# Softmax sums in the stage before the feed-forward on 32-column tiles, reciprocals taken of one column per transposed block, and weights converted without a clamp

## Chip, core and metric

The kernel runs on one core of a Trainium2 chip. A core has five engines with instruction streams of their own: TensorE (PE in the profile, its weight loads PEld), VectorE (DVE), ScalarE (ACT), GpSimd (POOL) and SyncE (SP), which here issues almost all DMAs. PE writes its products to PSUM, eight banks of 128 partitions; GpSimd doesn't reach PSUM in this kernel. The metric is the device time of one execution in microseconds, the median of several runs; lower is better.

## What is computed

Attention with RMS-normalized queries and keys over 8 batches of 12 heads (448 positions, head size 64), then a feed-forward with a squared ReLU over the 3584 rows that result. q, k and v are float32; the feed-forward's weights are float64 and reach the kernel as 64-bit words.

```python
def _attn_ref(q, k, v, g_q, g_k):
    def rmsnorm(x, g):
        rms = np.sqrt(np.mean(x * x, axis=-1, keepdims=True) + 1e-06)
        return x / rms * g
    q_n, k_n = (rmsnorm(q, g_q), rmsnorm(k, g_k))
    scores = 1.0 / np.sqrt(q.shape[-1]) * np.matmul(q_n, k_n.transpose(0, 1, 3, 2))
    scores = scores - np.max(scores, axis=-1, keepdims=True)
    attn = np.exp(scores)
    attn = attn / (np.sum(attn, axis=-1, keepdims=True) + 1e-09)
    return np.matmul(attn, v).astype(np.float32)

def _moe_ref(x, w_in, w_out):          # x: 3584 x 768, d_ff 2048
    h = np.maximum(x @ w_in, 0.0)
    return (h * h @ w_out).astype(np.float32)
```

## The kernel before

**Pairs.** The attention goes by pairs of heads: 8 batches of 6 pairs, 48 in all, numbered i. A pair's two heads (e = 0, 1) lie side by side on the 128 partitions. Its 448 keys are three slots m = 0, 1, 2 of 128 and a last one (m = NJ) of 64; the last slots of an even and the following odd pair share one tile. For each slot `weigh` makes transposed scores on PE (L369) into banks 0 to 3, and ACT takes the exponential into a tile wT (L374). `attend` multiplies the weights by v into the values bank (L438). The sums of the weights over the keys come in one of two ways. For pairs with `alone(i)`, those of the first two batches, every slot is also multiplied by a matrix of ones of 64 columns (L445), so that the sum stands on all 64 partitions of a head. For the others POOL adds the slots up (`add_up`, L393) and `denominators` multiplies the result once by ones (L456); ACT copies that out of bank 3 (L460). `invert_half` takes reciprocals on DVE, each of 128 x 224 elements, two per pair (L475), and `finish` multiplies the values by them (L484).

**Inputs of a pair.** q and k are loaded as rows, three per partition 128 rows apart (`load_full`, L147); squares on ACT (L167), sums on DVE (L178, L181), a power on POOL (L187), the scaling of q on POOL (L202); `turn` transposes q and k on PE (L344, L347), then DVE writes qT (L352) and ACT kT (L354). From pair 14 on, q and k come in blocks that DVE transposes (`turn_blocks`, L315). With gains as small as here the exponentials need no maximum; the branch with `shift` is for the other case and isn't taken.

**Feed-forward.** Two batches at a time, u = 0 to 3, in products of sums of blocks: `first_products` (L602, to L622 to L624) and `second_products` (L683, L654), whose results DVE adds to accumulators (L724, L700). A product is accumulated in one of three banks by roles, `roles`.

**Order.** There is no scheduler: the order of emission is that of each engine's queue. The outer loop goes through visits, two (n = 0, 1) for each pair. The first 26 are `visit_alone`, with attention alone on PE. In the first of them attend of the previous pair comes first, then the scores of this one, then a transpose; in the second attend again, the sums of squares, a transpose of k, the reciprocals and `finish`, and the scores. From then on the feed-forward's generator runs, and `visit_among` is called at even distances between its products; small jobs wait in `tasks` and `pool_tasks` and are emitted one or two per product. Thus everything that DVE does for attention stands in one queue with L724.

**Weights.** They come in 64 pieces. A piece is loaded by SP into a tile `words` (three buffers), split on ACT (L784 to L786) and joined on DVE: `join_words` first clamps the high words to plus or minus MOST (L797), then shifts them (L801); `end_join` follows with L821 and L825. 16 pieces go with the visits alone (`begin`), the other 48 with the first feed-forward (`convert`). From there on the forms of the weights are kept in DRAM.

**Banks** of the stage alone: scores 0 to 3; values 4 or 5 and sums 6 or 7, by the pair's parity (`values_bank`, `sums_bank`); the transposes use 4 to 7 too. Among the feed-forward: values 4, sums 3, transposes 0, products 5 to 7.

**Buffers**: wT has eight, acc seven (2*NT+1), part four; the squares of the stage alone lie in acc tiles, later in one tile `squares`.

## Time and profile before

| | us |
|---|---|
| median of 3 runs | 1480.34 (1480.28 to 1481.03) |
| the profiled execution | 1483.94 |
| its span, first to last instruction | 1482.0 |

Busy time of the engines over the span, and the costliest groups that the change touches (instructions, busy us, mean ns of one):

| | count | busy us | mean ns |
|---|---|---|---|
| PE | 4932 | 1447.8 (98%) | |
| DVE | 1225 | 744.7 (50%) | |
| ACT | 1151 | 606.6 (41%) | |
| POOL | 509 | 611.2 (41%) | |
| L475 reciprocals, source in SBUF | 72 | 108.6 | 1531 |
| L475 reciprocals, source in PSUM, 20 to 147 us | 22 | 32.6 | 1523 |
| L445 ones-products, 20 to 147 us | 144 | 34.2 | 539 |
| L445 with ones_of, 20 to 147 us | 48 | 11.1 | 539 |
| L797 clamps, 147 to 520 us | 48 | 27.7 | 578 |

A busy time is the union of a group's spans, so instructions that overlap count once. PE at 98% doesn't mean PE at its best: its matmuls are pipelined and their ends are modelled, so its pace is read from the starts. A float32 product shows as two MATMUL records and two weight loads. A row of the timeline is a run of like instructions of one engine, with the start of the first, the time from there to the end of the last, the names (out<-in), the shape and the count. "128\*64" is the tile of the array: rows by columns. An arrow in brackets names what ended the idle time before an instruction.

### The profile page before, as it was taken

Reading aid. Unit: us, or ns where it says so; the run is one execution under the profiler, and the core shown is the slowest. Engines: PE = TensorE matmul, PEld = TensorE weight load, DVE = VectorE, ACT = ScalarE, POOL = GpSimd, SP = SyncE. Lnnn points to the kernel's source line nnn. Section 1 sums busy time; section 2 is a strip of 40 time slices with the busy share of each in tenths; the row PEclk is TensorE's granted clock in tenths of the full one; section 3 lists DMA queues with packets and bytes.
Section 4 is the critical chain, followed back from the end, with each engine's and each line's share of the span. In section 5 each row is a group of like instructions: output and inputs, shape, how many; then the busy total and the mean of one; then the engine's idle time right before and its main releaser. Section 6 shows DMA issues by size and latency. Waiting matters only on the chain.

```text
span 1482.0 us, 15262 instructions
## 1 busy us (share of the span) xinstructions
PE 1447.8 (98%) x4932; PEld 691.5 (47%) x4932; DVE 744.7 (50%) x1225; ACT 606.6 (41%) x1151; POOL 611.2 (41%) x509
## 2 busy tenths in 40 slices
PE   7999999989999999999999999999999999999998
PEld 3333444444344444545444454544445455555554
DVE  5987367888887652335244353324434261222323
ACT  6775565645546334351433325342332403222130
POOL 3434745654635735354353645435352342021111
PEclk9999999999999999999999999999999999999999
DMA  6665336555646563443444464253533214223122
GB/s 150 166 191 136 75 83 179 163 179 147 203 128 210 166 209 89 127 130 63 147 102 137 119 193 126 55 163 86 144 103 109 81 69 166 85 75 122 38 85 77
DMA packets 309278, 188.11 MB, mean 127 GB/s; under 512 B 265796, under 2 KB 293316, under 8 KB 300996
## 3 DMA queue, kind: packets, MB, share of 16 engines
q1 hardware_dynamic: 308384, 186.84, 43.2%
q8 instruction: 41, 0.67, 0.2%
q14 instruction: 49, 0.40, 0.1%
q10 hardware_dynamic: 804, 0.20, 0.1%
HBM read 144.57 MB, written 42.40 MB: 126 GB/s over the span
## 4 chain that ended last, share of the span: by engine, by line
PE 89%; DVE 6%; DMA 1%; issue 1%; ACT 1%; SPq 0%; DVEq 0%; ACTq 0%
PE bank L602 33%; PE bank L683 28%; PE bank L369 9%; PE bank L438 9%; PE bank L654 5%; PE bank L445 2%; PE bank L456 2%; DVE xT L475 1%; DVE acc L724 1%; PE bank L344 1%; DVE words L797 1%; DVE hid L622 1%; DVE in_sb L801 0%; DMA vt<-in_v_dram 0%; ACT wT L374 0%
## 5 line engine op out<-in xcount | busy, mean ns | idle before, releaser
L602 PE MATMUL bank<-xT,in_sb 128*128 128x448 f32 x1344 | 517.3, 542 | 0.0
L602 PEld LDWEIGHTS bank<-xT,in_sb 128*128 128x128 f32 x1344 | 251.8, 190 | 262.1 <-issue 253.0
L724 DVE TENSOR_TENSOR acc<-acc,bank 128x384 f32<-128x384 f32 x324 | 172.0, 545 | 246.3 <-PE bank L683 186.8
L374 ACT ACTIVATE wT<-bank,rr 128x448 f32<-128x448 f32 x336 | 188.1, 633 | 260.6 <-PE bank L369 254.2
L683 PE MATMUL bank<-out_sb,hid 128*128 128x384 f32 x768 | 269.8, 491 | 7.5 <-DVE acc L724 7.4
L187 POOL TENSOR_TENSOR rr<-ms,minus_half 128x16 f32<-128x16 f32 (+3 forms) x50 | 125.4, 2508 | 352.2 <-DVE ms L181 322.9
L683 PE MATMUL bank<-out_sb,sums 128*128 128x384 f32 x576 | 207.4, 496 | 6.2 <-DVE acc L724 6.2
L622 DVE TENSOR_TENSOR hid<-bank,part 128x448 f32<-128x448 f32 x128 | 76.9, 621 | 271.9 <-PE bank L602 270.2
L683 PEld LDWEIGHTS bank<-out_sb,hid 128*128 128x128 f32 x768 | 144.9, 191 | 117.1 <-DVE acc L724 12.7
L393 POOL TENSOR_TENSOR sum<-sum,wT 128x448 f32<-128x448 f32 (+1 forms) x144 | 164.6, 1165 | 16.0 <-ACT wT L374 13.3
L369 PE MATMUL bank<-qT,kT 64*128 64x448 f32 (+1 forms) x768 | 166.2, 573 | 3.0 <-ACT words L784 1.1
L623 ACT ACTIVATE hid<-hid 128x448 f32<-128x448 f32 x128 | 73.3, 573 | 203.1 <-DVE hid L622 203.1
L683 PEld LDWEIGHTS bank<-out_sb,sums 128*128 128x128 f32 x576 | 108.3, 192 | 93.4 <-DVE acc L724 14.2
L638 POOL TENSOR_TENSOR sums<-hid 128x384 f32<-128x384 f32 x32 | 32.4, 1013 | 286.9 <-ACT hid L624 286.5
L438 PE MATMUL bank<-wT,vt 128*64 128x448 f32 x576 | 130.1, 548 | 1.5 <-DMA vt<-in_v_dram 1.5
L609 ACT COPY part<-bank 128x448 f32<-128x448 f32 x128 | 67.7, 529 | 149.0 <-PE bank L602 148.8
L475 DVE RECIPROCAL xT<-xT 128x224 f32<-128x224 f32 x72 | 108.6, 1531 | 28.4 <-ACT xT L460 28.4
L369 PEld LDWEIGHTS bank<-qT,kT 64*128 64x128 f32 (+1 forms) x768 | 54.9, 173 | 103.5 <-issue 82.2
L393 POOL TENSOR_TENSOR sum<-wT 128x448 f32<-128x448 f32 x72 | 83.6, 1181 | 45.8 <-PE bank L456 45.8
L178 DVE TENSOR_REDUCE ms<-squares 128x8 f32<-128x512 f32 (+1 forms) x68 | 41.9, 617 | 119.6 <-ACT squares L167 119.6
L654 PE MATMUL bank<-out_sb,hid 128*128 128x384 f32 x256 | 86.4, 491 | 0.0
L624 ACT ACTIVATE hid<-hid 128x448 f32<-128x448 f32 x128 | 73.8, 577 | 4.0
(70 smaller groups left out, 1115.4 us busy)
## 6 DMA issues: line engine op xcount, KB each, us to landing
out_sb<-out_forms SPq DMA_DIRECT2D x24, 1536.0 KB, 7.8
in_sb<-in_forms SPq DMA_DIRECT2D x24, 1344.0 KB, 5.9
words<-in_moe_w_in_dram SPq DMA_DIRECT2D x32, 384.0 KB, 3.6
words<-in_moe_w_out_dram SPq DMA_DIRECT2D x32, 384.0 KB, 3.4
out_forms<-out_sb SPq DMA_DIRECT2D x8, 1536.0 KB, 6.5
in_forms<-in_sb SPq DMA_DIRECT2D x8, 1344.0 KB, 5.7
qk<-in_q_dram SPq DMA_DIRECT2D x96, 96.0 KB, 3.2
vt<-in_v_dram SPq DMA_DIRECT2D x96, 96.0 KB, 3.4
```

Source lines behind the costliest of these rows:

```text
L187: self.nc.gpsimd.tensor_tensor(out=self.rr[i][:, first : first + number, 0 : self.count(i)], in0=ms, in1=self.minus_half[:, :, None].to_br ...
L369: nc.tensor.matmul(sc[some], lhsT=turned[p, 1][r, keys], rhs=turned[p, 0][r, :], start=True, stop=True,)
L374: nc.scalar.activation(new_weights((i, m), e), sc, AF.Exp, scale=rows.rr[i][:, 1, 2 * m + e : 2 * m + e + 1],)
L393: nc.gpsimd.tensor_tensor(out=sums[i, e][some], in0=left[some], in1=weights[key_of(i, m), e][some], op=ALU.add)
L438: nc.tensor.matmul(values_bank(i)[ds(e * D, D), :], lhsT=lasts[i % 2][some, e, :] if mine else values[i][:, m, e, :], rhs=weights[key, e][ ...
L475: nc.vector.reciprocal(out=dens[i][:, some], in_=den[:, some])
L602: nc.tensor.matmul(ps, lhsT=w_sb[:, IN.index(left), c, :], rhs=forms[u, c][right], start=first and c == 0, stop=c == NK - 1, skip_group_ch ...
L622: nc.vector.tensor_tensor(out=dst, in0=left, in1=right, op=op)
L624: nc.scalar.activation(dst, dst, AF.Square)
L654: nc.tensor.matmul(ps, lhsT=flat[a][:, t, ds(NT * P, P)], rhs=w_sb[t][:, 2 * a + half, :], start=(a, t) == parts[0], stop=(a, t) == parts[-1],
L683: nc.tensor.matmul(ps, lhsT=lefts[left][:, t, ts(tt, P)], rhs=w_sb[t][:, OUT.index(right), :], start=first and t == 0, stop=t == 1, skip_g ...
L724: nc.vector.tensor_tensor(out=acc, in0=acc, in1=ps, op=ALU.add)
```

## The change

Before the feed-forward the ones-products have 32 columns. The sums' bank then has four tiles of 32 partitions: for each head one that takes the first two slots in turn by their parity and one for the other parity. `attend` and the ones-products are separate functions now and go slot after slot; `visit_alone` emits scores first, then transposes, then the previous pair's products, and the pair's values always go to bank 4, its sums to bank 5, its transposes to 6 and 7. The weights of slots 0 and 1 of pairs alone lie in part and acc tiles, and the second square of such a pair is POOL's.

Reciprocals: DVE transposes the sums in blocks of 32 by 32 into a tile `inverse` (with the tag and the one buffer of `squares`), so that column 0 of each block holds 32 positions' sums on 32 partitions. Where the sums are in two parts, four copies of 32 partitions and an addition bring them together. The reciprocal is taken of 14 columns, and a transpose of its broadcast fills `inverse`, by which `finish` multiplies. Among the feed-forward the same is done after `denominators`, whose copy on ACT goes; transposing stands there at once, the rest is a task.

For pairs whose k isn't loaded in blocks, k and v are loaded with three adjacent rows on each partition (`in_chunks`). The clamp before the shift of the high words is left out. At the start of the first feed-forward two products are emitted ahead of the visit, and the roles of the banks begin in the order 7, 6, 5.

```diff
         ]
-    def go_on(self, io, small):
+        self.in_blocks = lambda i: False
+    def go_on(self, io, small, in_blocks):
+        other.in_blocks = in_blocks
         return other
+    def in_chunks(self, i, some):
+        if self.in_blocks(i):
+            return some.rearrange("(j p) d -> p j d", p=P)
+        return some.rearrange("(p j) d -> p j d", j=NJ)
...
     def load_full(self, i, x, queue):
         b, c = divmod(i, self.H // 2)
         for e in range(2):
+            some = self.qk[x][b, 2 * c + e, 0 : NJ * P]
             queue.dma_start(
                 self.part(i, x)[:, 0:NJ, e],
-                self.qk[x][b, 2 * c + e, 0 : NJ * P].rearrange("(j p) d -> p j d", p=P),
+                self.in_chunks(i, some) if x else some.rearrange("(j p) d -> p j d", p=P),
             )
...
             )
-    def square(self, i, x, room):
+    def square(self, i, x, room, engine=None):
         small = self.pools.small
         if i not in self.ms:
             self.ms[i] = small.tile([P, 2, 2 * NJ + 2], F32, name="ms", tag="ms")
             self.rr[i] = small.tile([P, 2, 2 * NJ + 2], F32, name="rr", tag="rr")
         squares = room.rearrange("p (r d) -> p r d", d=self.D)[:, 0 : self.count(i)]
-        self.nc.scalar.activation(squares, self.flat(i, x), AF.Square)
+        qk = self.flat(i, x)
+        if engine is None:
+            self.nc.scalar.activation(squares, qk, AF.Square)
+        else:
+            engine.tensor_tensor(out=squares, in0=qk, in1=qk, op=ALU.mult)
         self.squares[i, x] = squares
...
     def turn(i, x):
-        tr = banks[6 - 2 * x + (i - 1) % 2 if i < 2 or alone(i - 2) else 0]
+        tr = banks[6 + x if i < 2 or alone(i - 2) else 0]
         dst = att.tile([P, S], F32, name="qT" if x == 0 else "kT")
         for j in range(NJ):
             nc.tensor.transpose(
...
         turned[i, x] = dst
     def new_weights(n, e):
-        weights[n, e] = att.tile([P, S], F32, name="wT", tag="wT", bufs=8)
+        i, m = n
+        if m < 2 and alone(i) and not shift:
+            weights[n, e] = new_acc()[:, 0:S] if m else new_part()
+        else:
+            weights[n, e] = att.tile([P, S], F32, name="wT", tag="wT", bufs=8)
         return weights[n, e]
...
                     nc.vector.tensor_copy(out=tiles[n][e][:, part], in_=tr[:, n, :size])
                 nc.vector.tensor_copy(out=tiles[NJ][e][mine, part], in_=tr[mine, NJ, :size])
-    def values_bank(i):
-        return banks[4 + i % 2 if alone(i) else 4][:, 0:S]
     def sums_bank(i):
-        return banks[6 + i % 2 if alone(i) else 3][:, 0:S]
-    def attend(i, m, first, last):
-        key, mine = key_of(i, m), m == NJ
-        some = ds(i % 2 * LASTS, LASTS) if mine and shift else ds(0, P)
+        return banks[5 if alone(i) else 3][:, 0:S]
+    def attend(i, some):
+        order = values_of(i)
+        for n in some:
+            m = order[n]
+            mine = ds(i % 2 * LASTS, LASTS) if m == NJ and shift else ds(0, P)
+            for e in range(2):
+                nc.tensor.matmul(
+                    banks[4][ds(e * D, D), 0:S],
+                    lhsT=lasts[i % 2][mine, e, :] if m == NJ else values[i][:, m, e, :],
+                    rhs=weights[key_of(i, m), e][mine], start=n == 0, stop=n == NJ,
+                )
+    def add_weights(i, some):
+        order = values_of(i)
+        for n in some:
+            m = order[n]
+            mine = ds(i % 2 * LASTS, LASTS) if m == NJ and shift else ds(0, P)
+            for e in range(2):
+                nc.tensor.matmul(
+                    sums_bank(i)[ds(e * D + n % 2 * SIDE, SIDE), :],
+                    lhsT=ones_of[i % 2][mine] if m == NJ else ones[:, 0:SIDE],
+                    rhs=weights[key_of(i, m), e][mine], start=n < 2, stop=n >= 2,
+                )
+    def forget(i, some):
+        for n in some:
+            m = values_of(i)[n]
+            if m < NJ or i % 2 or shift:
+                for e in range(2):
+                    del weights[key_of(i, m), e]
+    def denominators(i):
         for e in range(2):
             nc.tensor.matmul(
-                values_bank(i)[ds(e * D, D), :],
-                lhsT=lasts[i % 2][some, e, :] if mine else values[i][:, m, e, :],
-                rhs=weights[key, e][some], start=first, stop=last,
+                sums_bank(i)[ds(e * D, D), :], lhsT=ones, rhs=sums.pop((i, e)),
+                start=True, stop=True,
             )
-        for e in range(2):
-            if alone(i) or shift:
-                nc.tensor.matmul(
-                    sums_bank(i)[ds(e * D, D), :], lhsT=(ones_of[i % 2] if mine else ones)[some],
-                    rhs=weights[key, e][some], start=first, stop=last,
-                )
-            if not mine or i % 2 or shift:
-                del weights[key, e]
-    def denominators(i):
-        den = sums_bank(i)
-        for e in range(2):
-            nc.tensor.matmul(
-                den[ds(e * D, D), :], lhsT=ones, rhs=sums.pop((i, e)), start=True, stop=True
-            )
-        dens[i] = new_x()
-        nc.scalar.copy(dens[i], den)
+        take_sums(i)
+    def take_sums(i):
+        inverse[i] = io.tile([P, S], F32, name="inverse", tag="squares", bufs=1)
+        nc.vector.transpose(inverse[i], sums_bank(i))
     def invert(i):
-        if shift or alone(i):
-            dens[i] = new_x()
-            den = sums_bank(i)
-        else:
-            den = dens[i]
+        columns = inverse[i].rearrange("p (t n) -> p t n", n=SIDE)
+        few = columns[:, :, 0:1]
+        new_few = lambda: small.tile([P, S // SIDE, 1], F32, name="few", tag="few", bufs=3)
+        if alone(i) or shift:
+            other, both = new_few(), new_few()
+            for n in range(P // SIDE):
+                nc.vector.tensor_copy(out=other[ts(n, SIDE)], in_=few[ts(n ^ 1, SIDE)])
+            nc.vector.tensor_tensor(out=both, in0=few, in1=other, op=ALU.add)
+            few = both
         if shift:
-            nc.vector.tensor_scalar(out=dens[i], in0=den, scalar1=1e-9, scalar2=None, op0=ALU.add)
-            den = dens[i]
-        return den
-    def invert_half(i, half, den):
-        some = ds(half * (S // 2), S // 2)
-        nc.vector.reciprocal(out=dens[i][:, some], in_=den[:, some])
+            nc.vector.tensor_scalar(out=few, in0=few, scalar1=1e-9, scalar2=None, op0=ALU.add)
+        by = new_few()
+        nc.vector.reciprocal(out=by, in_=few)
+        nc.vector.transpose(columns, by.to_broadcast([P, S // SIDE, SIDE]))
+    def new_part():
+        return ffn_p.tile([P, S], F32, name="part", tag="part", bufs=4)
     def new_x():
         return ffn_p.tile([P, S], F32, name="xT", tag="xT", bufs=11 * NK - 1)
...
     def finish(i):
         b, c = pairs[i]
-        xT = dens.pop(i)
-        nc.vector.tensor_tensor(out=xT, in0=values_bank(i), in1=xT, op=ALU.mult)
-        xts[b, c] = xT
+        xts[b, c] = new_x()
+        nc.vector.tensor_tensor(
+            out=xts[b, c], in0=banks[4][:, 0:S], in1=inverse.pop(i), op=ALU.mult
+        )
         for x in range(2):
             del turned[i, x]
         del values[i]
...
         if n in words:
             high = words[n][:, :, 1]
             nc.vector.tensor_scalar(
-                out=high.bitcast(F32), in0=high.bitcast(F32), scalar1=MOST, scalar2=-MOST,
-                op0=ALU.min, op1=ALU.max,
-            )
-            nc.vector.tensor_scalar(
                 out=dst.bitcast(U32), in0=high, scalar1=4, scalar2=1,
                 op0=ALU.logical_shift_left, op1=ALU.logical_shift_right,
             )
...
         elif n:
             weigh_shifted(i)
+    def attend_all(i):
+        slots = range(NJ + 1)
+        attend(i, slots)
+        add_weights(i, slots)
+        forget(i, slots)
+        take_sums(i)
+        invert(i)
+        finish(i)
     def visit_alone(i, n):
         step = i * 2 * VISITS + 2 * n
-        visit(i, n)
-        if n:
+        if n == 0:
+            load_v(i)
+            if i and shift:
+                attend_all(i - 1)
+            weigh_slots(i, n)
+            turn(i + 1, 1)
+            turn(i + 1, 0)
+            square(i + 2, 0, new_acc())
+            square(i + 2, 1, new_acc(), nc.gpsimd)
+            begin(step)
+            if i and not shift:
+                attend(i - 1, range(NJ))
+                add_weights(i - 1, (0, 1))
+                forget(i - 1, (0, 1))
+        else:
             normalize(i + 2)
-            if i == 0:
-                turn(1, 0)
-            turn(i + 1, 1)
-            if not alone(i) and not shift:
+            weigh_slots(i, n)
+            begin(step)
+            if in_blocks(i + 2):
                 store_q(i + 2)
                 load_blocks(i + 2, 0)
                 load_blocks(i + 2, 1)
             load_qk(i + 4)
             if i and not shift:
-                invert_all(i - 1)
+                attend(i - 1, (NJ,))
+                add_weights(i - 1, (2, 3))
+                forget(i - 1, (2, 3))
+                take_sums(i - 1)
+                invert(i - 1)
                 finish(i - 1)
-        begin(step)
-        weigh_slots(i, n)
-        if n and not alone(i) and not shift:
-            additions(i)
-        if n == 0:
-            if i:
-                turn(i + 1, 0)
-            for x in range(2):
-                square(i + 2, x)
+            if not alone(i) and not shift:
+                additions(i)
         begin(step + 1)
...
     def visit_among(i, n):
         run_tasks(len(tasks) + len(pool_tasks))
-        visit(i, n)
+        if not shift:
+            if n and i - 1 not in inverse:
+                denominators(i - 1)
+            attend(i - 1, (2 * n, 2 * n + 1))
+            forget(i - 1, (2 * n, 2 * n + 1))
+        elif n == 0:
+            attend_all(i - 1)
+        if n == 0 and i <= last:
+            load_v(i)
         if i <= last:
             weigh_slots(i, n)
         if n and not shift:
-            den = invert(i - 1)
-            tasks.append(lambda: invert_half(i - 1, 0, den))
-            tasks.append(lambda: invert_half(i - 1, 1, den))
+            tasks.append(lambda: invert(i - 1))
             tasks.append(lambda: finish(i - 1))
         if n and i <= last and not shift:
             additions(i)
         if n == 0 and i + 2 <= last:
-            square(i + 2, 0, True)
+            room = io.tile([P, 4 * P], F32, name="squares", tag="squares", bufs=1)
+            square(i + 2, 0, room)
             tasks.append(lambda: None)
             tasks.append(lambda: rows.add(i + 2, 0))
-            tasks.append(lambda: square(i + 2, 1, True))
+            tasks.append(lambda: square(i + 2, 1, room))
             tasks.append(lambda: rows.add(i + 2, 1))
             tasks.append(lambda: pool_tasks.append(lambda: put_in_order(i + 2)))
             if in_blocks(i + 2):
...
                     stream, spent, first = ffn(u + 1), 0, u < 0
                     if shift:
                         run(COST)
+                    elif first:
+                        run(COST_IN + 1)
                 visit_among(i, n)
         run(COST)
         drain()
```

## What the change is predicted to do

> **What bounds the kernel now.** I first read the busy time by stretch (columns: length; busy time and count of PE, weight loads, DVE, ACT, POOL; granted TensorE clock; DMA share; GB/s), cut where the work changes: attention alone to 147 us, then the first feed-forward, in which the weights are still converted, to about 520, then the other three.
>
> ```profile
> 20.00:147.00 127.00, 124.94 (x658) 48.57 (x656) 103.00 (x167) 85.86 (x165) 54.70 (x36) 1.00 0.60 164
> ...
> 200.00:520.00 320.00, 304.07 (x982) 139.45 (x981) 253.32 (x411) 171.87 (x336) 173.71 (x136) 0.98 0.58 167
> 520.00:1400.00 880.00, 880.00 (x2859) 434.00 (x2859) 330.84 (x546) 296.94 (x554) 331.54 (x285) 1.00 0.38 115
> ```
>
> From 520 us PE never rests and DVE is 38% busy: nothing that eases DVE is worth anything there. Only the first row and the second have time to give. Twelve pairs in the first row's 127 us are 10.6 us a pair.
>
> The timeline of PE tells what fills such a pair (start, duration, group):
>
> ```profile
> 60.52 1.94 PE L369 MATMUL bank<-qT,kT 64*128 64x448 f32 x12
> 62.39 0.97 PE L438 MATMUL bank<-wT,vt 128*64 128x448 f32 x4
> 63.19 0.92 PE L445 MATMUL bank<-wT,ones 128*64 128x448 f32 x4
> 63.94 0.92 PE L438 MATMUL bank<-wT,vt 128*64 128x448 f32 x4
> 64.69 0.92 PE L445 MATMUL bank<-wT,ones 128*64 128x448 f32 x4
> 65.54 1.77 PE L369 MATMUL bank<-qT,kT 64*128 64x448 f32 x8
> 67.25 0.55 PE L344 MATMUL bank<-wide,qk 128*128 128x128 f32 x3
> ```
>
> Starts are to be read, since ends are modelled. From 63.19 to 63.94 to 64.69 each group of four takes 0.75 us: four records are two column tiles, each with two records per product, so two 64-column tiles run side by side in 0.375 us a step. The groups follow each other without a hole: this stretch is PE's. The odd groups pay for a change of tile shape: 65.54 less 64.69 is 0.85, not 0.75, and four steps of L369, at 0.375, take 1.71, not 1.50: about 0.1 us before a switch and 0.1 behind it.
>
> In the feed-forward the waits list (total, times, longest) has one large entry for PE, and DVE's timeline shows what stood ahead of the awaited L724:
>
> ```profile
> PE bank L683 <- DVE acc L724: 13.6, 11, 3.0
> ```
>
> ```profile
> 289.96 1.15 DVE L797 TENSOR_SCALAR words<-words 128x384 f32<-128x384 f32 x1
> 291.14 1.05 DVE L801 TENSOR_SCALAR in_sb<-words 128x384 uint32<-128x384 uint32 x1
> 292.12 1.54 DVE L475 RECIPROCAL xT<-xT 128x224 f32<-128x224 f32 x1
> 293.58 0.99 DVE L821 SCALAR_TENSOR_TENSOR in_sb<-words,in_sb 128x384 uint32<-128x384 uint32 x1
> 294.71 1.13 DVE L825 CUSTOM_DVE_ANT_0 in_sb<-words,in_sb 128x768 uint16<-128x768 uint16 x1
> 295.76 1.54 DVE L475 RECIPROCAL xT<-xT 128x224 f32<-128x224 f32 x1
> 297.23 0.49 DVE L724 TENSOR_TENSOR acc<-acc,bank 128x384 f32<-128x384 f32 x1
> ```
>
> The wait that ended at 297.8 is the 3.0. Of the 7.3 us of queue ahead of L724, 4.2 are two reciprocal halves and one limit pass. Behind such stalls the granted clock fell:
>
> ```profile
> 360.00:400.00 40.00, 36.93 (x116) 16.38 (x115) 36.37 (x52) 24.76 (x49) 28.23 (x22) 0.98 0.58 157
> 400.00:440.00 40.00, 37.63 (x116) 17.59 (x116) 32.27 (x62) 14.35 (x28) 13.10 (x11) 0.89 0.56 168
> ```
>
> 0.02 and 0.11 of 40 us are 5.2 us lost.
>
> **The ones-products.** Twelve pairs by 4 slots by 2 heads by 2 records are the 192 MATMULs of L445: two wide, 96 steps by 0.375, 36 us. The change makes tiles of 32 columns, two heads by two slots, so that four can run at once: 48 steps, 18 us, a gain of 18. The trace has no 32-column tile. The nearest row is the 64-by-64 scores, eight records in two steps:
>
> ```profile
> 61.47 0.98 PE L369 MATMUL bank<-qT,kT 64*64 64x448 f32 x8
> ```
>
> The next group starts at 62.39, 0.92 later, 0.46 a step with a switch in it: four tiles do run at once, but on two row halves, with two streams per partition where the change asks for four. Bounds: 18 if all four run, 0 if two do; not below 0, as the step count cannot grow. The Trainium skill ("TensorE: Matmul & The Clock Gate", Part 3) gives 2.38x for three 32-column tiles, 79% of ideal; a step of 0.375/0.79 = 0.47 would leave a gain of 13. The row of two 64-column tiles shows no such loss (0.375 each), so I take 18.
>
> **Against it** stands a rule of the Trainium skill ("TensorEngine Tiling (Array Packing)", Key Properties): changing the tiling mode drains TensorE. Now values and ones share one mode. Before, two pairs pass through 13 changes (counted in the timeline from 60.52 to 81.73); afterwards each of four visits is scores, (transposes or quarter scores,) values, ones: 15. One more a pair, 12 by 0.2 us measured above: 2.4 us back. Taken by the rule alone, without a price, a drain of the 0.54 us that a MATMUL lasts would make it 6.5, an estimate. The row decides: net gain 15.6, or 1.3 a pair, so PE alone would need 9.3.
>
> **One bank for values, one for sums.** Before, banks 4/5 and 6/7 alternate by pair; now every pair alone uses 4 and 5, and the next values product waits for L484's successor in finish. A loop appears. PE: three slots of values 2.25, two slots of ones 0.75, scores of the second visit 1.15 on average, values 0.75, ones 0.75, four switches 0.8: 6.45. Then the DVE chain: 0.25 until DVE starts (as L475 after L445), transpose, four copies, sum, reciprocal, transpose, multiply. Transposes: L315 is the same form from SBUF,
>
> ```profile
> L315 DVE STREAM_TRANSPOSE kT<-qk x34: 631/634/645, 160.3 to 1133.9; 128x448 f32<-128x448 f32 x34
> ```
>
> so 0.63 each. The six small ones have no row: not under 0.06 (the 128x1 memset at the start), near L181's 0.17 on 128x6, so 0.36 to 1.0 together; I take 0.8, as a reciprocal of 14 columns costs 14/224 of 1.53, 0.1, above the fixed part. Multiply 0.62. Chain 0.25+0.63+0.8+0.63+0.62 = 2.95; loop 9.4. Beside it PE has scores 1.5, transposes 0.86 and switches to do, so it stalls hardly at all with DVE free. But queued ahead of the first transpose on DVE are this visit's reductions (two, 0.61 mean, with two L181) and perhaps a weight piece (1.5 us); 1.67 pieces a pair fall here. DVE per pair: 103/12 = 8.6 now, less 3.05 reciprocals, less 0.63 (7.6 us of L797 by 12), plus 0.63+0.8+0.63: 7.0 of 9.4, so it usually arrives in time. I allow 0.4 a pair: cycle 9.8, gain **9.6 us** over twelve; ends 15.6 (no stall) and about 1 (a whole piece ahead every time, cycle 10.5).
>
> **Reordered visits and buffers.** Scores now come ahead of the previous pair's values, both transposes follow the first scores. The first wait of PE for L352's qT (0.7 us at 19.08) goes, as qT is then asked for a visit earlier. POOL takes one square of each pair: near L202 on the same shape, 1.04 us, beside 54.7 busy in 127, so hidden unless its power instruction (2.9) stands ahead; then the reduction, and the transpose queued behind it, come late, which the 0.4 contains. ACT loses it, 0.59 of 7.2 a pair. On SP the v loads stay at the head of the first visit, and values are asked for after scores and transposes, some 2.4 us later than before; k and v as three adjacent rows are one run of 768 instead of three of 256 bytes. PE waited 2.0 us for v; I leave them in. Weights in acc and part rooms free wT slots: no wait for them is in PE's list. So +0.7 in all.
>
> **First feed-forward.** DVE loses 48 limit passes, 27.7 us, and on each of 12 pairs 3.05 of reciprocals for 1.26 of transposes and 0.2: 19; together 47 of its 253. The largest block that can stand before L724 shrinks from 1.54 to 0.63. What is late next is the conversion chain (L801, L821, L825: 3.2 us at 290), so I keep 2.6 of the 13.6 and 0.7 of the 5.2 clock loss: gain 11.0 + 4.5 = **15.5**. Ends: 7 and 20. Two products run ahead of visit 13: the same work, earlier, 0.
>
> **Later stages.** ACT's copy (L460, 0.51) of bank 3 becomes the DVE transpose, 0.63, in a queue 38% busy. PE's next writer of bank 3 is slot 3, behind two slots of values (1.5) and slot 2 (0.75): 2.25 us of cover. Without it, up to 0.6 a pair. The inverse takes the squares' buffer, so ACT's square waits for finish: scores' exponentials, 2.1 us, stand before it. 0, ends -5 and +3.
>
> **Sum**: -9.6 - 0.7 - 15.5 = -25.8. The profiled run took 1483.94 us (span 1482.0, 1.9 around it), the median of the three timed is 1480.34; the difference of 3.6 I carry over: **1455 us**.
>
> **Rivals.**
> (a) Only two 32-column tiles run at once. For it: no such row. Alone then costs +2.4 and the loop is covered: 1480.3 + 2.4 - 0.7 - 15.5 = 1466.5.
> (b) The loop binds at about one piece a pair, cycle 10.5: -1.2 - 16.2, 1463. For it: DVE shows 19 of 20 us busy between 40 and 60. Against: it sheds 1.6 a pair.
> (c) Slower: the same stage, with reductions that wait for POOL's square and a piece both ahead of the first transpose on DVE, 3.1 us every pair: cycle 12.5, 12 by 1.9 = +22.8, less 16.2: 1487. It decides against the change from a cycle of 12.0, 2.5 us of queue each pair. Against: DVE would be 7.0 of 12 busy.
> (d) Nothing changes: the passes removed were never late. PE's list of waits speaks against it. 1480.
> (e) All these stalls go: -15.6 - 0.7 - 18.8, 1445.
>
> **How the numbers follow.** Forecast 0.58, (a) 0.13, (b) 0.14, (c) 0.06, (d) 0.02, (e) 0.07. Own range of the forecast 1447 to 1462. With (a), (b) and (e) in, 1443 to 1470. A difference of 0.2%, 3 us, is about what this measurement tells from none. Faster 0.92, same 0.02, slower 0.06.
>
> **What would show it.** In the profile after: 32-column ones-products whose group of eight starts 0.75 us before the next group (1.5 says (a)); pairs alone 9.8 us apart; PE's waits for the inverse's multiply below 6 us; L683 waiting less than 4 us for accumulators and a clock of 1.00 from 360 to 440; an unchanged rate from 520 on. I am wrong if pairs stay above 10.4 us apart or if PE waits for DVE beyond 520.

## The result and the profile after

| | before | changed |
|---|---|---|
| median, us | 1480.68 (4 runs, 1480.28 to 1481.32) | 1462.24 (4 runs, 1460.26 to 1463.95) |
| profiled execution, us | 1483.94 | 1461.41 |
| its span, us | 1482.0 | 1459.6 |

The ratio is 0.9875, with a 95% interval from 0.9858 to 0.9892: faster by 18.4 us. The forecast was 1455, faster by 25.8. The two spans lie 22.4 apart, as the profiled execution of before was 3.6 above the median of the first three runs and that of the changed kernel 0.8 below its own; the stages below share out the 22.4. Executions of one kernel differ by a few us with the clock that they were granted: those of before that took 1483.9 us or more, the profiled one among them, show a mean of 0.996, those below 1481 show 0.998; the changed kernel took 1460.26 at 1.000 and 1463.95 at 0.996.

Two marks cut both traces at the same work: the start of the multiply in `finish` of pair 11, the last pair alone, and the start of the first product of the second feed-forward.

| us | before | changed | difference | forecast |
|---|---|---|---|---|
| start to the multiply of pair 11 | 150.6 | 150.9 | +0.3 | -10.3 |
| from there to the second feed-forward | 381.1 | 360.6 | -20.5 | -15.5 |
| from there to the end | 950.4 | 948.1 | -2.3 | 0 |

The stage at which most of the edits aim gained nothing; the first feed-forward gave all of it and more. The busy times by stretch of the changed kernel, columns as before:

```profile
20.00:147.00 127.00, 114.03 (x671) 38.97 (x669) 96.23 (x218) 80.66 (x156) 68.39 (x49) 0.99 0.60 165
200.00:520.00 320.00, 315.24 (x1038) 146.88 (x1037) 225.29 (x389) 172.09 (x334) 178.71 (x140) 1.00 0.62 182
520.00:1400.00 880.00, 880.00 (x2859) 436.44 (x2858) 295.36 (x563) 283.66 (x526) 324.05 (x280) 1.00 0.38 113
```

PE fell from 124.94 to 114.03 busy us in the first row, while the row's work takes as long: work turned into waiting. In the second row PE holds 1038 matmuls instead of 982. The list of what PE waited for up to 520 us says the same:

```profile
PE bank L455 <- DVE xT L524: 8.7, 7, 3.2
PE bank L357 <- POOL qk L216: 3.5, 5, 1.0
PE bank L724 <- DVE acc L765: 3.0, 4, 1.3
```

Before, PE's whole list from 20 to 147 us was two loads of v:

```profile
PE bank L438 <- DMA vt<-in_v_dram: 1.5, 1, 1.5
PE bank L438 <- DMA lasts<-in_v_dram: 0.5, 1, 0.5
```

The waits for accumulators fell from 13.6 to 3.0 us. Two lines that before did not have stand above them: the values products (now L455) wait for the multiply of `finish` (L524), and the transposes of q (L357) for POOL's scaling (L216). The granted clock, which had been 0.98 and 0.89 between 360 and 440 us, is full there:

```profile
360.00:400.00 40.00, 37.95 (x127) 17.16 (x124) 29.37 (x49) 23.78 (x48) 22.15 (x18) 1.00 0.61 182
400.00:440.00 40.00, 39.54 (x133) 18.10 (x133) 31.05 (x60) 21.43 (x42) 22.88 (x18) 1.00 0.62 182
76.00:82.00 6.00, 5.22 (x22) 1.52 (x24) 4.19 (x10) 0.54 (x1) 1.45 (x1) 0.72 0.99 317
```

The third row shows it down in a new place, just behind the longest of the new waits. (A drop can follow such a wait but need not: the run with rows 128 apart, below, pauses for 3.15 us at the same place, and its clock is 1.00 there.) That wait is worth reading. PE's timeline around it (start, duration, group):

```profile
67.19 0.57 PE L468 MATMUL bank<-part,ones 128*32 128x448 f32 x2
67.20 0.57 PE L468 MATMUL bank<-acc,ones 128*32 128x448 f32 x2
67.59 0.55 PE L468 MATMUL bank<-part,ones 128*32 128x448 f32 x2
67.60 0.55 PE L468 MATMUL bank<-acc,ones 128*32 128x448 f32 x2
68.08 1.02 PE L387 MATMUL bank<-qT,kT 64*128 64x448 f32 x4
...
73.36 0.27 PE L360 MATMUL bank<-wide,qk 128*128 128x128 f32 x1
76.78 0.60 PE L455 MATMUL bank<-wT,lasts 128*64 128x448 f32 x2 [3.15 <-DVE xT L524]
```

The first four rows settle the tiles: four products of 32 columns start within 0.02 us of each other, and the eight records take 0.89 us to the next group, with a switch of tile shape in it. Before, the ones-products of two slots took 1.60, also with a switch (0.75 and 0.85, by the starts in the prediction's rows). The last row is PE, through with all that doesn't need the values bank, idle for 3.15 us. DVE and POOL meanwhile:

```profile
71.37 0.64 DVE L496 STREAM_TRANSPOSE inverse<-bank 128x448 f32<-128x448 f32 x1
72.05 2.85 DVE L505 COPY few<-inverse 32x14 f32<-32x14 f32 x4
74.94 0.18 DVE L506 TENSOR_TENSOR few<-inverse,few 128x14 f32<-128x14 f32 x1
75.15 0.24 DVE L511 RECIPROCAL few<-few 128x14 f32<-128x14 f32 x1
75.42 0.65 DVE L512 STREAM_TRANSPOSE inverse<-few 128x448 f32<-128x448 f32 x1
76.10 0.62 DVE L524 TENSOR_TENSOR xT<-bank,inverse 128x448 f32<-128x448 f32 x1
```

```profile
72.09 0.83 POOL L216 TENSOR_TENSOR qk<-qk,rr 128x384 f32<-128x384 f32 x1
72.88 0.99 POOL L884 TENSOR_TENSOR in_sb<-in_sb 128x384 f32<-128x384 f32 x1
73.84 1.03 POOL L181 TENSOR_TENSOR acc<-qk 128x512 f32<-128x512 f32 x1
```

Four copies of 14 columns took 2.85 us: the first 0.16, the others 0.72, 0.95 and 0.98. By the trace these three end at 72.94, 73.91 and 74.90 us, and POOL's three instructions at 72.92, 73.87 and 74.87: each copy came out just behind one of them. Not every instruction of POOL does this: 20 copies of other pairs ran beside its power (L201) and took 0.163 to 0.171 us.

### The profile page after: what moved, and what is told of

Its sections match the earlier page's. It is cut to its first block, busy times and chain, and to the rows that moved or that the text cites. A ratio compares the mean times of both kernels' runs of the same rounds, so it can differ in the third digit from the quotient of the medians.

```text
span 1459.6 us, 15299 instructions
## 1 busy us (share of the span) xinstructions
PE 1425.6 (98%) x4932; PEld 680.2 (47%) x4932; DVE 667.3 (46%) x1269; ACT 583.7 (40%) x1102; POOL 623.2 (43%) x522
## 4 chain that ended last, share of the span: by engine, by line
PE 90%; DVE 4%; issue 3%; POOL 2%; ACT 1%; DMA 1%; SPq 0%; POOLq 0%; DVEq 0%; ACTq 0%
PE bank L643 35%; PE bank L724 29%; PE bank L455 9%; PE bank L387 8%; PE bank L695 5%; PE bank L485 2%; PE bank L468 1%; POOL rr L201 1%; DMA qk<-in_q_dram 1%; DVE few L505 1%; POOL qk L216 0%; DVE inverse L512 0%; DVE out_sb L884 0%; DVE xT L524 0%; DVE acc L765 0%
## 5 line engine op out<-in xcount | busy, mean ns | idle before, releaser
L392 ACT ACTIVATE wT<-bank,rr 128x448 f32<-128x448 f32 x288 | 161.1, 631 | 269.1 <-PE bank L387 249.1
L201 POOL TENSOR_TENSOR rr<-ms,minus_half 128x16 f32<-128x16 f32 (+3 forms) x50 | 125.7, 2514 | 333.1 <-DVE ms L195 299.1
L724 PE MATMUL bank<-out_sb,sums 128*128 128x384 f32 x576 | 204.0, 490 | 3.1 <-DVE acc L765 3.0
L724 PEld LDWEIGHTS bank<-out_sb,hid 128*128 128x128 f32 x768 | 144.8, 190 | 107.2 <-issue 6.8
L411 POOL TENSOR_TENSOR sum<-sum,wT 128x448 f32<-128x448 f32 (+1 forms) x144 | 164.3, 1164 | 12.8 <-ACT wT L392 10.4
L455 PE MATMUL bank<-wT,vt 128*64 128x448 f32 x480 | 106.2, 546 | 0.0
L695 PEld LDWEIGHTS bank<-out_sb,hid 128*128 128x128 f32 x256 | 47.6, 190 | 39.3 <-issue 5.7
```

The costliest lines, as they stand in the source:

```text
L201: self.nc.gpsimd.tensor_tensor(out=self.rr[i][:, first : first + number, 0 : self.count(i)], in0=ms, in1=self.minus_half[:, :, None].to_br ...
L392: nc.scalar.activation(new_weights((i, m), e), sc, AF.Exp, scale=rows.rr[i][:, 1, 2 * m + e : 2 * m + e + 1],)
L411: nc.gpsimd.tensor_tensor(out=sums[i, e][some], in0=left[some], in1=weights[key_of(i, m), e][some], op=ALU.add)
L455: nc.tensor.matmul(banks[4][ds(e * D, D), 0:S], lhsT=lasts[i % 2][mine, e, :] if m == NJ else values[i][:, m, e, :], rhs=weights[key_of(i, ...
L695: nc.tensor.matmul(ps, lhsT=flat[a][:, t, ds(NT * P, P)], rhs=w_sb[t][:, 2 * a + half, :], start=(a, t) == parts[0], stop=(a, t) == parts[-1],
L724: nc.tensor.matmul(ps, lhsT=lefts[left][:, t, ts(tt, P)], rhs=w_sb[t][:, OUT.index(right), :], start=first and t == 0, stop=t == 1, skip_g ...
```

## Experiments

All are the changed kernel with one edit, but for the two that combine edits and for the last, which is the kernel before. Each was timed beside before; the ratios to it are what compares best, and differences of some 2 us between medians are within what the clock does. "Stage" is the time to the multiply of pair 11, by the trace.

| kernel | median us | ratio to before, 95% | stage us |
|---|---|---|---|
| changed | 1462.24 | 0.9875 (0.9858 to 0.9892) | 150.9 |
| ones on 64 columns | 1460.42 | 0.9856 (0.9841 to 0.9870) | 148.2 |
| two banks for values | 1459.98 | 0.9849 (0.9836 to 0.9861) | 149.8 |
| copies as sums | 1456.40 | 0.9829 (0.9817 to 0.9842) | 145.2 |
| square on ACT | 1459.25 | 0.9848 (0.9835 to 0.9860) | 146.1 |
| ones before values | 1456.86 | 0.9833 (0.9819 to 0.9846) | 147.2 |
| that, and copies as sums | 1451.72 | 0.9799 (0.9785 to 0.9812) | 140.6 |
| all three | 1450.71 | 0.9793 (0.9780 to 0.9807) | 138.0 |
| rows 128 apart | 1460.21 | 0.9858 (0.9842 to 0.9873) | 149.7 |
| clamp back | 1474.55 | 0.9952 (0.9936 to 0.9967) | 157.7 |
| former reciprocals | 1471.29 | 0.9928 (0.9912 to 0.9943) | 152.0 |
| no products ahead | 1467.23 | 0.9901 (0.9883 to 0.9919) | 150.7 |
| before without clamp | 1471.01 | 0.9925 (0.9911 to 0.9940) | 149.3 |

### The stage alone: is it held by the one values bank?

**Ones on 64 columns.** One slot at a time on tiles of 64; the four copies and the addition go, since the sum is whole. (The small tile `few` has one buffer instead of three, for room, and `ones_of` has 64 columns too.)

```diff
-                    sums_bank(i)[ds(e * D + n % 2 * SIDE, SIDE), :],
-                    lhsT=ones_of[i % 2][mine] if m == NJ else ones[:, 0:SIDE],
-                    rhs=weights[key_of(i, m), e][mine], start=n < 2, stop=n >= 2,
+                    sums_bank(i)[ds(e * D, D), :],
+                    lhsT=ones_of[i % 2][mine] if m == NJ else ones,
+                    rhs=weights[key_of(i, m), e][mine], start=n == 0, stop=n == NJ,
```

> Ones-products on 64 columns again, one slot at a time, in the changed order and with the changed reciprocals; the four copies and the addition across partitions go with it. Theory L: PE does 1.5 us more a pair, but the chain on DVE is 1.2 us shorter and PE has more to do beside it, so most of it is paid by waits that vanish: slower by 0 to 6 us. Rival (PE's work is what counts, 32 columns saved their 15.6 us): slower by 13 to 18 us.

Measured: 1460.42, not slower at all (the intervals of the ratios overlap). PE's whole list of waits for 20 to 147 us, and its busy time there:

```profile
PE bank L357 <- DMA qk<-in_q_dram: 0.9, 1, 0.9
```

```profile
20.00:147.00 127.00, 126.09 (x673) 49.09 (x671) 81.81 (x164) 80.75 (x157) 70.34 (x50) 1.00 0.60 165
```

Both waits are gone, and PE is full again. Without copies and addition the chain on DVE from L496 to the end of L524 takes 2.26 us in the mean of the twelve pairs, against 3.64 in the changed kernel. So what the narrow tiles took from PE, they gave back. By the starts of PE's records over the same eleven pairs (in the changed kernel from the transposes at 21.8 us to those at 138.6), they take 15.7 us off the ones-products; 8.6 us come back as waits before values products, 4.4 among the transposes, 2.2 in switches between values on 64 columns and ones on 32 (0.1 each), and 1.6 as loss of clock: 1.1 more than was saved. The rival that PE's work counts falls.

**Copies as sums.** The same four copies in another form, a reduction over an axis of one element.

```diff
-                nc.vector.tensor_copy(out=other[ts(n, SIDE)], in_=few[ts(n ^ 1, SIDE)])
+                nc.vector.tensor_reduce(
+                    out=other[ts(n, SIDE), :, 0], in_=few[ts(n ^ 1, SIDE)], axis=AX.X, op=ALU.add
+                )
```

> The four copies of 32 partitions take 0.16 us on DVE beside an idle POOL and 0.72 to 0.98 us beside a POOL instruction (mean 0.26). Written as sums over an axis of one element they should keep to 0.17 to 0.21 if it is the copy's form that POOL holds up. Theory L: the chain from the sums to finish gets 0.3 us shorter in the mean and over 2 us in the worst pair; the time falls by 3 to 5 us. If the copies aren't what makes the chain long: less than 1 us.

Measured: 1456.40. The groups of the changed kernel and of this one, from 20 to 147 us (count, busy us, mean ns, idle before):

```profile
L505 DVE COPY few<-inverse 32x14 f32<-32x14 f32 x44 | 11.4, 260 | 1.1
```

```profile
L505 DVE TENSOR_REDUCE few<-inverse 32x14 f32<-32x14 f32 x48 | 8.1, 168 | 1.2
```

None takes over 0.173 us now, where the copies went up to 0.984; the chain falls to 3.30 us, PE's wait for `finish` from 8.7 to 5.3. The clock doesn't drop at 77 us in this execution, where the 3.15 us pause is gone: by the starts over the same eleven pairs, 3.4 us of the gain are shorter waits before values products and 1.6 are clock. So it was the copy's form that POOL held up. The addition behind it (L508) is not free of this: it took up to 0.70 us here, ending just behind an instruction of POOL's.

**Two banks for values.** Even pairs' values in bank 7, odd ones' in 4; q is transposed into the sums' bank 5, k into 6.

```diff
-        tr = banks[6 + x if i < 2 or alone(i - 2) else 0]
+        tr = banks[5 + x if i < 2 or alone(i - 2) else 0]
+    def values_bank(i):
+        return banks[7 if alone(i) and i % 2 == 0 else 4]
```

> Theory L (the stage alone is held by the loop through the one values bank: PE's products of values wait for finish, 11.0 us of PE's time by the starts): with the values of even pairs in bank 7, odd ones in bank 4, the transposes of q in the sums' bank 5 and those of k in bank 6, PE's waits of L455 for L524's successor go and the time falls by 7 to 11 us, to 1451 to 1455. Rival A (ACT or the input DMAs hold the stage at 10.7 us a pair): another wait takes its place, less than 3 us. Rival P (POOL's chain power, scaling, square holds it): waits of the transposes for POOL's scaling grow by what the values give up, less than 3 us.

Measured: 1459.98, a miss. PE's waits up to 147 us:

```profile
PE bank L357 <- POOL qk L216: 6.1, 8, 2.1
PE bank L471 <- DVE qT L365: 4.3, 3, 2.3
```

The wait for `finish` is gone, as theory L has it, but two others took its place. One is of my own making: the ones-products (L471) now wait until qT has left their bank, and qT stands on DVE behind the same chain. The other is POOL, longer by 2.6. And the clock was halved twice for 3.4 us in this execution. So the bank alone isn't the bound; behind it stands DVE's queue and, next to it, POOL.

**Square on ACT.** `square(i + 2, 1, new_acc(), nc.gpsimd)` without its last argument.

> The second square of a pair alone goes back to ACT. Theory P (POOL's square delays its power and scaling, for which the transposes of q wait 5.8 us, and holds up DVE's small copies): the time falls by 3 to 6 us. Rival A (ACT is the bound of the stage, 0.59 us a pair more): the time rises by 3 to 7 us. Theory L alone: within 2 us.

Measured: 1459.25, 3.0 better by the medians, though the interval just touches that of the changed kernel. PE's wait for L216 fell from 3.5 to 1.9 us. ACT is not the bound: it has 88 of 127 us.

**Ones before values.** The sums come first in both visits, so that the chain starts earlier and the bank is wanted later.

```diff
-                attend(i - 1, range(NJ))
                 add_weights(i - 1, (0, 1))
+                attend(i - 1, range(NJ))
...
-                attend(i - 1, (NJ,))
                 add_weights(i - 1, (2, 3))
+                attend(i - 1, (NJ,))
```

> The changed kernel with the ones-products ahead of the values in both visits, nothing else. Theory L (the chain from the sums through DVE to finish is longer than what PE has to do until the next values product, by 0.9 us a pair in the mean): the chain starts 0.85 us earlier and the next use of the values bank comes 0.85 us later, so most of the 11 us of PE's wait for finish goes: faster than the changed kernel by 5 to 9 us, 1453 to 1457. Rival P (behind that wait stands POOL's scaling of q): 0 to 3 us, and the transposes' waits for POOL grow instead.

Measured: 1456.86. The wait for `finish` fell from 8.7 to 3.1 us, that for POOL rose from 3.5 to 4.7: L's range, with a share of rival P. What is left of the first are three waits of up to 2.3 us, where copies were held up by POOL again (three of the twelve chains took over 4.7 us), with two clock drops behind.

**That, and copies as sums.**

> The same with the four copies as sums over one element as well. Theory L: the waits for finish are gone by the order already, or nearly, so the two don't add: 0 to 3 us better than the order alone, 1451 to 1455. Were they independent, they'd add to 11 to 15.

Measured: 1451.72. They add, 5.4 and 5.8 to 10.5: my expectation that they'd overlap was wrong. The order covers the chain's mean length, the form cuts its outliers (the longest chain takes 4.1 us, with the order alone 5.4), and the waits for `finish` needed both:

```profile
PE bank L357 <- POOL qk L216: 5.5, 6, 1.4
PE bank L726 <- DVE acc L767: 3.0, 4, 1.3
PE bank L387 <- ACT qT L330: 1.6, 3, 0.7
PE bank L455 <- DVE xT L526: 0.2, 1, 0.2
```

What POOL holds up in the chain is now the addition, up to 0.98 us in one pair. The first row is the changed kernel, the second this run:

```profile
L506 DVE TENSOR_TENSOR few<-inverse,few 128x14 f32<-128x14 f32 x11 | 1.9, 176 | 0.4
L508 DVE TENSOR_TENSOR few<-inverse,few 128x14 f32<-128x14 f32 x12 | 4.4, 369 | 0.4
```

With the order changed it costs PE nearly nothing, as the last wait of the list, 0.2 us, shows.

**All three.**

> The same with the second square of a pair back on ACT. With finish out of the way POOL is what PE waits for next (5.8 us before the transposes): another 2 to 4 us better than without, 1448 to 1452. Rival A (ACT has 0.59 us more a pair and becomes the bound): slower than without by 1 to 4.

Measured: 1450.71, the fastest here, 11.5 us below the changed kernel; 1.0 below the run without the third edit, less than the 2 to 4 expected and not told apart by the interval, though the stage is 2.6 shorter. The wait for POOL falls to 3.5.

**Rows 128 apart.** `in_chunks` always takes the former pattern.

> The changed kernel with k and v loaded as before, rows 128 apart. I took the form of the loads to be worth 0.7 us or less: within 1.5 us of the changed kernel. Rival: runs of 256 bytes keep the queues so busy that the values come late, 3 us or more slower.

Measured: 1460.21, no slower; the 2.0 below the changed kernel are no gain of this edit that the interval would tell. The page of the changed kernel has the same packets as that of before, to the last one, and so has this run:

```profile
DMA packets 309278, 188.11 MB, mean 129 GB/s; under 512 B 265796, under 2 KB 293316, under 8 KB 300996
```

### The first feed-forward: which edit gave the 20 us?

**Clamp back.** The instruction of L797 again ahead of the shift.

> The changed kernel with the clamp of the high words put back before the shift. Theory D (DVE's queue before the accumulators was the whole of the first feed-forward's loss, and each of its three reliefs counts by its busy time): 27.7 of the 47 us taken off DVE there come back, so 8 to 12 of the 20 us that this stage gained are lost, and 1 to 5 in the stage alone, where 0.5 us a piece returns to a DVE queue that is late already: slower than the changed kernel (1462) by 9 to 16 us. Rival R (it is the 1.5 us blocks of the reciprocals that stall PE, single passes of 0.35 to 0.58 don't): slower by 0 to 4.

Measured: 1474.55. By the traces 6.9 us are lost in the stage alone, 3.4 of them because the clock lost 5.1 us there instead of 1.7, and 6.2 behind it (12.3 by the medians); PE's wait for accumulators is 6.5 instead of 3.0. Theory D has the total but not the split: the 16 passes in the stage alone cost more than the 48 behind it.

**Former reciprocals** among the feed-forward, with ACT's copy.

```diff
-        take_sums(i)
+        inverse[i] = new_x()
+        nc.scalar.copy(inverse[i], sums_bank(i))
...
-            tasks.append(lambda: invert(i - 1))
+            tasks.append(lambda: invert_half(i - 1, 0))
+            tasks.append(lambda: invert_half(i - 1, 1))
```

> The changed kernel with the former reciprocals for the pairs among the feed-forward alone: ACT's copy of bank 3 and two reciprocals of 128 x 224. Theory D: 19 of the 47 us come back, slower than the changed kernel by 6 to 10 us, all of it before 520 us; nothing beyond. Rival R: slower by 11 to 18. Rival S (the later stages gain from the copy that ACT lost): another 1 to 3 us beyond 520.

Measured: 1471.29. Between the marks 7.7 us are lost, D's range, and the wait for accumulators is 9.4; beyond, 2.0, as rival S had it: the last row of the stage table. Whether ACT's copy or DVE's time makes these 2.0 was not tried.

**No products ahead.** The two lines with `run(COST_IN + 1)` left out.

> The changed kernel without the two products ahead of visit 13. If the order is all that changes, as I took it: within 1.5 us of the changed kernel. Rival: PE has nothing to do there while the last pairs alone are finished, and up to 4.5 us, the time of two products, are lost.

Measured: 1467.23, 5.0 lost, 5.7 between the marks. PE's wait for `finish` up to 520 us is 12.9 instead of 8.7 (the longest 4.2), and the clock is halved for 3.4 us at 152, which is 1.7 of the 5.7. The values of pair 12 need bank 4, which pair 11's multiply frees; the two products are what PE does meanwhile.

**Before without clamp.** The kernel before, without L797.

> The kernel before, without the clamp and else untouched. Theory D: faster than before by 6 to 11 us, of them 1 or less before 150 us, where PE has no wait for DVE. Rival R: by 0 to 4.

Measured: 1471.01, 10.7 less than before (1481.67 beside it): 1.2 in the stage alone, 11.6 between the marks. The wait for accumulators fell from 13.6 to 8.1, and the two drops of the clock, 5.2 us, didn't occur.

Undone one at a time, clamp, reciprocals and products ahead give back 6.2 + 7.7 + 5.7 = 19.6 of the 20.5 us between the marks. That they nearly make up the whole is in part chance: the clamp alone was worth 11.6 in the kernel before and 6.2 in the changed one, so what an edit is worth depends on the others, and the clock drops in or out of each execution.

## Why the prediction was right, and where it was not

**What held.** The bound by stages, and that relief for DVE is worth something before 520 us only, up to the 2.3 us beyond. Four tiles of 32 columns do run at once, as I took from the 64-column row; they go at 0.40 us a step. A step of 0.47, the prediction's estimate from the 2.38x for three tiles in the Trainium skill ("TensorE: Matmul & The Clock Gate", Part 3), was too long here. The ones-products lost 15.7 us over eleven pairs, 17 for twelve, where I had 18, and the switches cost the 0.2 a pair of my term. The clock loss of the first feed-forward went with its stalls. The accumulator waits ended at 3.0, where I kept 2.6.

**Where it failed by its own signs.** I had written that I am wrong if pairs stay above 10.4 us apart: they came 10.7 apart, not 9.8. PE's waits for the multiply are 8.7 us where they should stay below 6. So the account of the stage alone was wrong: a gain of 10.3 was forecast and none came. The other sign, PE waiting for DVE beyond 520, didn't show. The total of 1462.24 lies at the upper end of my range, 1447 to 1462, and nearer to rival (b)'s 1463 than to 1455.

**The step that failed** is the chain of "One bank for values, one for sums": 0.25 until DVE starts and 2.7 from the first transpose to the multiply, 2.95, with 0.4 a pair for what stands ahead. Measured, L496 starts 0.72 us after the last ones-record, 0.34 after its 0.375 us step, and L496 to the end of L524 takes 3.64 us: 3.98. The transposes (0.65 each) and the multiply were right. The six small instructions, which I put at 0.8 between ends of 0.36 and 1.0, took 4 by 0.27, 0.18 and 0.24, 1.48 in all, and all hand-overs in the chain 0.24. By the starts of its matmuls PE lost 9.4 us before values products, counted above the 0.20 from the last transpose that stands there when nothing waits: over twelve pairs 0.8 each, most of the 1.0 that the chain was underestimated by.

The 0.17 of a neighbouring row was the wrong price for a copy, since L181 has its length beside an idle POOL. The Trainium skill ("SBUF — State Buffer", Who interferes with whom) has the rule that I should have weighed: a DVE copy can take the port pair that it shares with GpSimd, is then blocked for a whole instruction of the other, and a reduction never is. The trace and the run with reductions agree: up to 0.98 against 0.173 us. That copies beside POOL's power were not held, I can't explain from these runs. And the change itself had moved a POOL instruction, the square, into that place.

**Rival (b)** named the right loop and nearly its cycle, but not its cause. Not a weight piece stood ahead of the chain; DVE was there first in ten of the twelve pairs, idle for the sums:

```profile
L496 DVE STREAM_TRANSPOSE inverse<-bank 128x448 f32<-128x448 f32 x11 | 7.1, 649 | 17.3 <-PE bank L468 17.2
```

**POOL's square**, which I called hidden but for what the 0.4 contains, was the second term: 3.5 us of waits, and 1.6 of them go with the square. **The two products ahead**, put at 0, were worth 5.0, because I asked what they move and not what PE would wait for at that place. **The loads** by adjacent rows gave nothing; "one run of 768" bytes is not what the queues carried.

**What is luck in the total.** These errors partly cancel: 10.6 too much in the first stage, 5.0 and 2.3 too little in the others. Of the 7.4 us missing by the medians only 3.4 are left by the traces. Most of the other 4.0 is a mistake in my last line: it takes 4.5 us of clock loss out of the profiled execution and then carries over the 3.6 by which this execution was slower than the median, though that is clock too (0.996 against 0.998 of 1482 us are 3 us, an estimate). Counted once, the forecast is about 1458.

DVE's total in the stage is 8.0 us a pair (96.23 by 12) where I had 7.0. Of these 12 us 6.4 are the six small instructions; 4.0 are that the row of before holds the reciprocals of eleven pairs (22, 32.6 us) and I took off those of twelve; and 2.4 are L195, which grew from 4.0 to 6.4 us, as single ones took up to 0.98.

What stays open: why a wait of PE is followed by a drop of the clock in one execution and not in another, and whether ACT's copy or DVE's time makes the 2.0 us that the former reciprocals cost beyond the second mark.

## What to carry to other kernels

When a buffer that alternated becomes a single one, add up the chain that frees it, instruction by instruction with hand-overs, and set it against what the fast engine can do meanwhile; an edit that takes work off that engine shortens the cover by the same amount. Put first on the fast engine what starts such a chain: here the ones-products before the values gave 5 us for exchanging two pairs of lines. In such a chain, price small instructions by what runs beside them, and choose a form that a neighbour can't hold up, for each of them: when the copies were safe here, the addition behind them was held.

## What the runs showed of the hardware

A copy of 32 x 14 elements on DVE takes 0.16 to 0.17 us beside an idle POOL and beside POOL's power; one that started beside its scaling, square or joining (L216, L181, L884) ended just behind POOL's instruction, after up to 0.98 us. As a reduction it takes 0.162 to 0.175 in every run that has it. An addition of 128 x 14 takes 0.18 and was held in the same way, up to 0.99 (all three edits).

Eight records on four 32-column tiles go in two steps of 0.40 us, where 64-column tiles take 0.375, and going from tiles of 64 to 32 columns adds 0.1 us (0.469 between the starts instead of 0.369).

One pause of PE of 3.15 us was followed by 3.4 us at half the clock, so that it cost 1.7 us more than its own length; one of the same length in the run with rows 128 apart was not. In before, two pauses of 2.2 us were followed by 6.8 and 3.4 us at half the clock, and one of 3.0 us by none.

Three adjacent rows of 256 bytes per partition gave not one packet less than three rows 128 apart.
